# Attention scores from unsplit factors in one run of eight matmuls, and the state step joined to the output step

## The chip, the cores and the metric

The kernel runs on one core of a Trainium2 chip. The metric is the time of one execution in device microseconds, as the median of several runs. TensorE (PE in the profile, PEld for its weight loads) does the matmuls, VectorE (DVE), ScalarE (ACT) and GpSimd (POOL) work on tiles in the on-chip memory, and SyncE (SP) issues the DMAs.

## What is computed

Three layers follow each other: a linear attention with a decaying state, a mixture of four experts weighted by given probabilities, and a second mixture of eight experts to which each row is routed. The change touches the attention alone:

```python
def _attn_ref(r, k, v, w, u) -> np.ndarray:      # batch 4, heads 8, seq 768, head_dim 48
    ...
    for t in range(S):
        kt, vt, rt = (k[:, :, t], v[:, :, t], r[:, :, t])
        cur = np.einsum('bhd,bhe->bhde', u[None] * kt, vt)
        y[:, :, t] = np.einsum('bhd,bhde->bhe', rt, state + cur)
        state = w[None, :, :, None] * state + np.einsum('bhd,bhe->bhde', kt, vt)
```

The first mixture is `p[:, e] * (relu(x @ w1[e]) @ w2[e])` summed over its four experts, for 3072 rows of 384 with a hidden size of 1024.

## The kernel before

**The attention** is done in 24 chunks, six for each of the four batch entries. A chunk is 128 positions of all eight heads, which lie as four pairs; the two heads of a pair lie in the partitions 0 to 63 and 64 to 127 of the transposed factors. `attn_steps` gives the steps of one chunk. `mul` scales the loaded transposed r and k by powers of w, `rk`, `ru`, `kn` and `cv` on POOL and `cc` on DVE make the term with u and the scaled k. `scores` multiplies k by r for each head into two PSUM tiles, `am` (DVE) copies these under the causal mask, `y_mm` multiplies by v and adds the part of the state before, `x_add` (DVE) adds the term with u, `state` makes the next state (four matmuls, then on DVE an addition and a multiplication), and `tr` transposes the chunk's x and splits it on ACT and DVE into the two parts of `XT`, which the first mixture multiplies.

Chunks 0 to 5 take the scores from the factors as they are, in float32 and over the 48 rows of a head: eight matmuls (line 968). The trace shows each of these as two records. Chunks 6 to 23 first split both factors into a high and a low part (`k_parts` on DVE and POOL, `r_parts` on ACT and DVE) and take three products of parts over 64 rows: 24 matmuls (line 963).

**The first mixture** is the bulk of PE's work. It runs as 32 units: for each of 16 pairs of batch entry and expert, two blocks of 384 rows. A unit is `up` (72 matmuls of 384 columns, lines 1133 to 1137, three for each of eight hidden blocks times three) and then `down` (72 more, lines 1154 to 1158). After each hidden block ACT and DVE split the result into the two parts of h (lines 1141, 1142). Unit 0 multiplies the rows of chunks 0 to 2, unit 1 those of chunks 3 to 5.

**What sets the order.** The attention steps are strewn between these matmuls by program order. `tick()` is called after every third matmul, so 48 times in a unit, 24 of them in `up`. Every third tick takes one step from `queue`; in unit 0 a second one is taken on the ticks between while more than 11 steps wait. Chunks 3 to 5 are queued for unit 0. At the start of the units 1 to 6, 9 to 14 and 17 to 22 what is left in the queue is done at once by `flush()`, and one chunk, 6 to 23, is queued. So step number n of such a chunk stands behind tick 3n of its unit: the first behind hidden block 0, the eighth at the end of `up`, the ninth and tenth in `down`. Every engine works through its instructions in this order and waits only for the data.

Of the kernel before, what the change touches and what calls it, by code (L numbers as in the profile page):

```python
# [8 lines left out]
F32 = mybir.dt.float32  # L9
F32R = mybir.dt.float32r  # L10
BF = mybir.dt.bfloat16
I32 = mybir.dt.int32
AF = mybir.ActivationFunctionType
OP = mybir.AluOpType
# [617 lines left out]
def rwkv_moe_moe(ctx, tc, A, out):  # L632
# [104 lines left out]
    with tc.If(chunked > 0) as cmp:  # L737
        main(tc, A, out, C, False)
    with cmp.Else():
        main(tc, A, out, C, True)  # L740
# [74 lines left out]
def main(ctx, tc, A, out, C, stepwise):  # L815
    nc = tc.nc
# [6 lines left out]
    at = att_ctx.enter_context(tc.tile_pool(name="at", bufs=1))  # L823
# [3 lines left out]
    ld = {}  # L827
# [66 lines left out]
    ps = {}  # L894
# [3 lines left out]
    def attn_steps(ck, detail=False):  # L898
        c = ck % 6
        b = ck // 6  # L900
        split_scores = ck >= 6

        def mul(engine, p0=0, p1=4):
            t, n = ld[ck]
            engine.tensor_tensor(t[:, :, p0:p1], t[:, :, p0:p1], tp[:, :, p0:p1, 0:128], op=OP.mult)

        def rk():
            t, n = ld[ck]
            r, k = n[:, 0:384], n[:, 768:1280].rearrange("p (h d) -> p h d", h=8)
            r3 = r.rearrange("p (h d) -> p h d", h=8)  # L910
            nc.gpsimd.tensor_tensor(r3, r3, k[:, :, 0:48], op=OP.mult)

        def ru():
            r = ld[ck][1][:, 0:384]
            nc.gpsimd.tensor_tensor(r, r, u_b, op=OP.mult)

        def kn():
            t, n = ld[ck]
            nc.gpsimd.tensor_tensor(n[:, 768:1280], n[:, 768:1280], pkn.rearrange("p a b -> p (a b)"), op=OP.mult)

        def pre():
            rk()
            ru()
            kn()
# [14 lines left out]
            cc()  # L939
            cv()  # L940


        def k_parts():
            t, n = ld[ck]
            nc.vector.tensor_copy(Kb[:, 0], t[:, 1])
            nc.gpsimd.tensor_tensor(Kb[:, 1], t[:, 1], Kb[:, 0].bitcast(F32), op=OP.subtract)

        def r_parts():
            t, n = ld[ck]
            nc.scalar.activation(Rb[:, 0], t[:, 0], AF.Copy)  # L950
            nc.vector.tensor_sub(Rb[:, 1], t[:, 0], Rb[:, 0].bitcast(F32))

        def scores(p0, p1):
            t, n = ld[ck]
            if p0 == 0:
                ps[ck] = [psum.tile([128, 4, 128], F32, name="at", bufs=4) for _ in range(2)]
            if split_scores:

                for p in range(p0, p1):
                    for n, (a, b) in enumerate(((0, 0), (0, 1), (1, 0))):  # L960
                        for s in range(2):
                            q = slice(64 * s, 64 * s + 64)
                            nc.tensor.matmul(ps[ck][s][:, p, :], Kb[q, a, p], Rb[q, b, p], start=n == 0, stop=n == 2)  # L963
                return
            for p in range(p0, p1):
                for s in range(2):
                    q = slice(64 * s, 64 * s + 48)
                    nc.tensor.matmul(ps[ck][s][:, p, :], t[q, 1, p, :], t[q, 0, p, :], start=True, stop=True)  # L968

        def am(p0=0, p1=4):  # L970
            if p0 == 0:
                st[ck] = at.tile([128, 2, 4, 128], F32, name="am", bufs=1)
            for s in range(2):
                nc.vector.tensor_mul(st[ck][:, s, p0:p1], ps[ck][s][:, p0:p1],
                                     mask[:, None, :].to_broadcast([128, p1 - p0, 128]))

        def att():
            scores(2, 4)
            am()

        def yy():
            y_mm()
            x_add()

        def y_mm():
            t, n = ld[ck]
            v = n[:, 384:768]
            y = psum.tile([128, D], F32, name="at", bufs=4)
            for p in range(4):
                if c:  # L990
                    nc.tensor.matmul(y[:, 96 * p:96 * p + 96], t[:, 0, p, :], S[ck - 1][:, p, :],  # L991
                                     start=True, stop=False)
                for s in range(2):
                    h = 2 * p + s
                    nc.tensor.matmul(y[:, 48 * h:48 * h + 48], st[ck][:, s, p, :],  # L995
                                     v[:, 48 * h:48 * h + 48],
                                     start=not c, stop=bool(s) or not c)
            st[ck] = y

        def x_add():  # L1000
            x = at.tile([128, D], F32, name="x", bufs=2)
            nc.vector.tensor_add(x, st[ck], ld[ck][1][:, 0:384])
            st[ck] = x
# [36 lines left out]
        nothing = lambda: None  # L1040
        if stepwise:
            return [fetch, nothing, nothing, nothing, nothing, nothing, tr]
        if detail:
            return dict(mul=mul, rk=rk, ru=ru, kn=kn, cc=cc, cv=cv, scores=scores, am=am, y=y_mm, x=x_add, state=state, tr=tr)
        if not split_scores:
            return [lambda: (mul(nc.vector), pre()), pre2, lambda: scores(0, 2), att, yy, state, tr]
        return [lambda: mul(nc.gpsimd), k_parts, r_parts, pre, pre2, lambda: scores(0, 2), att, yy, state, tr]

    if not stepwise:
        Rb = at.tile([128, 2, 4, 128], F32R, name="Rb")  # L1050
        Kb = at.tile([128, 2, 4, 128], F32R, name="Kb")


    W1, W2 = {}, {}
# [205 lines left out]
    def enqueue(ck, tail=0):  # L1260
        s = attn_steps(ck)

        def head():
            if 4 <= ck + 1 < NCK:
                load_chunk(ck + 1)
            s[0]()
        queue.append(head)
        queue.extend(s[1:])
# [5 lines left out]
    if stepwise:  # L1274
# [5 lines left out]
        for ck in range(3):  # L1280
            for f in attn_steps(ck):
                f()
        for f in range(8):
            split(1, f, wl[0])
    else:
# [20 lines left out]
        def w128_in():  # L1306
            w128 = C["w128"]
            nc.vector.tensor_mul(w128, tp[:, 0, :, 128:129], tp[:, 0, :, 128:129])
            for s in range(2):
                r = slice(64 * s, 64 * s + 48)  # L1310
                nc.vector.tensor_copy(w128m[r, :, 48 * s:48 * s + 48], w128[r].to_broadcast([48, 4, 48]))

        a, b, c = (attn_steps(ck, True) for ck in range(3))
        a["mul"](nc.gpsimd, 0, 1)
        a["mul"](nc.gpsimd, 1, 2)
# [56 lines left out]
    for ui, (i, blk) in enumerate(units):  # L1372
        b, e = runs[i]
# [204 lines left out]
    for ph in range(E2):  # L1578
        a, b, c = route.phase(ph == E2 - 1, name_job, start_job, 20 if ph == 0 else None)
# [9 lines left out]
    def tick1(j):  # L1589
        clk[0] += 0.161  # L1590
        if len(job) > j + 2:
            return
        due = lambda q: q and clk[0] >= ready[q is search]

        hold = due(search) and not (number and not job)
        if due(number) and (not number[0][1] or not search or len(job) < j + 2 or hold and search[0][1]):
            pop_route(number)
            if hold and search and search[0][1]:
                pop_route(search)
        elif hold:  # L1600
            pop_route(search)

    def tick2(j):
        tick1(j)
        take_names()
        for q in known[j:j + 2]:
            prepare(q, "loads")
        for q in job[j:j + 2]:
            if q["rows"] and rows_there:
                prepare(q, "rows")  # L1610
                break
# [13 lines left out]
    while len(job) < 1 or job[0]["rows"]:  # L1625
        n = min([jb["rows"][0][2]() for jb in job[:1]] + [ready[x is search] for x in (number, search) if x])
# [12 lines left out]
    for j in range(E2):  # L1639
# [27 lines left out]
        t, t1 = lambda: tick2(j), lambda: tick1(j)  # L1667
# [54 lines left out]
```

## Time and profile before

| | |
|---|---|
| median of 3 runs | 1244.8 us (1244.26 to 1245.34) |
| the profiled execution | 1240.1 us, its span in the trace 1238.1 us |
| PE busy | 1213.8 us, 98% of the span |
| VectorE, ScalarE, GpSimd busy | 51%, 23%, 33% |
| the units with a chunk of split scores | 18 of 32 |
| one matmul of 384 columns, start to start | 0.173 us |

A PE that is busy for 98% of the span does not yet say that every microsecond is needed: a busy time is the union of overlapping records, and a record is longer (0.34 us) than the distance to the next (0.17 us). What a step costs on PE is read from starts: from the last matmul of the mixture ahead of it to the second one behind it, less the two distances that would lie there without the step. The second one is taken, because behind a step the first starts, and then the second still comes late.

### The profile page before, as it was taken

The page shows a single profiled execution, that of the slowest core. Times are in us where ns is not written, and L with a number is a line of the kernel's source. Part 1 is how long each engine was busy: PE and PEld are TensorE (multiplying, and loading weights), DVE is VectorE, ACT ScalarE, POOL GpSimd, SP SyncE. Part 2 cuts the span into 40 slices and gives each one's busy share as a digit, 9 for nine tenths or more (in the row PEclk, how much of TensorE's full clock was granted, in tenths as well). Part 3 has the DMA queues.
Part 4 walks back from the last instruction along what each step waited for, and adds up shares of the span by engine and source line. Part 5 has one row for each costly group of instructions (what it writes and reads, how often), then busy time and mean ns, then how long its engine had stood idle before and what let it go on. Part 6 is the DMA issues. An engine that isn't in the chain of part 4 may idle for free.

```text
span 1238.1 us, 21280 instructions
## 1 busy us (share of the span) xinstructions
PE 1213.8 (98%) x7986; PEld 1174.4 (95%) x7986; DVE 629.5 (51%) x1667; ACT 287.2 (23%) x608; POOL 412.0 (33%) x413
## 2 busy tenths in 40 slices
PE   8999999999999999999999999999999999999995
PEld 8899999999999999999999999999998888899995
DVE  7643333367333334863333369279674766663320
ACT  1322222211222222232222222223211011222221
POOL 5555454511444444234444433222200012122210
PEclk7899999999999999999999999999999999999998
DMA  6676555433777777477777655779730486667770
GB/s 250 209 258 241 199 182 201 141 122 121 246 255 256 254 257 258 159 246 272 248 260 251 231 170 172 256 262 317 247 119 18 152 281 230 221 223 267 283 287 27
DMA packets 95929, 267.65 MB, mean 216 GB/s; under 512 B 11328, under 2 KB 15552, under 8 KB 95680
## 3 DMA queue, kind: packets, MB, share of 16 engines
q1 hardware_dynamic: 92736, 256.67, 60.1%
q0 software_dynamic: 3072, 9.44, 2.1%
q8 instruction: 67, 1.10, 0.4%
q14 instruction: 54, 0.44, 0.1%
HBM read 181.13 MB, written 84.93 MB: 215 GB/s over the span
## 4 chain that ended last, share of the span: by engine, by line
PE 89%; issue 4%; DMA 2%; DVE 2%; POOL 1%; ACT 0%; POOLq 0%; DVEq 0%; ACTq 0%
PE mm L1133 13%; PE mm L1154 13%; PE mm L1156 13%; PE mm L1158 13%; PE mm L1135 13%; PE mm L1137 12%; PE at L995 3%; PE at L963 2%; PE at L991 2%; DMA acc<-x2d,idx 1%; PE at L1012 1%; PE at L471 1%; PE at L1028 1%; POOL out_dram L1661 1%; PE at L968 1%
## 5 line engine op out<-in xcount | busy, mean ns | idle before, releaser
L1133 PE MATMUL mm<-xT,w 128*128 128x384 f32 x960 | 327.5, 341 | 0.6 <-ACT xT L1544 0.6
L1135 PE MATMUL mm<-xT,w 128*128 128x384 f32 x960 | 322.8, 336 | 0.2
L1137 PE MATMUL mm<-xT,w 128*128 128x384 f32 x960 | 322.3, 336 | 0.0
L1154 PE MATMUL mm<-w,h 128*128 128x384 f32 x939 | 320.5, 341 | 0.9 <-DMA w<-w2s 0.9
L1156 PE MATMUL mm<-w,h 128*128 128x384 f32 x939 | 315.8, 336 | 0.0
L1158 PE MATMUL mm<-w,h 128*128 128x384 f32 x939 | 315.5, 336 | 0.0
L1141 ACT ACTIVATE h<-mm 128x384 fp32r<-128x384 f32 x313 | 153.9, 492 | 529.2 <-PE mm L1137 487.2
L1142 DVE SCALAR_TENSOR_TENSOR h<-mm,h 128x384 fp32r<-128x384 f32 x313 | 173.7, 556 | 197.1 <-ACT h L1141 195.9
L1073 POOL TENSOR_TENSOR ws<-raw,ws 128x384 fp32r<-128x384 f32 x128 | 135.2, 1062 | 345.3 <-ACT ws L1072 345.2
L1133 PEld LDWEIGHTS mm<-xT,w 128*128 128x128 f32 x960 | 180.3, 188 | 4.4 <-ACT xT L1544 0.8
L1135 PEld LDWEIGHTS mm<-xT,w 128*128 128x128 f32 x960 | 180.4, 188 | 1.2 <-DVE xT L1545 0.8
L1137 PEld LDWEIGHTS mm<-xT,w 128*128 128x128 f32 x960 | 180.3, 188 | 0.1
L1154 PEld LDWEIGHTS mm<-w,h 128*128 128x128 f32 x939 | 176.6, 188 | 1.7 <-ACT ws L1072 1.2
L1156 PEld LDWEIGHTS mm<-w,h 128*128 128x128 f32 x939 | 176.6, 188 | 0.9 <-issue 0.4
L1158 PEld LDWEIGHTS mm<-w,h 128*128 128x128 f32 x939 | 176.3, 188 | 0.4
L1170 DVE SCALAR_TENSOR_TENSOR scr<-acc,wg 128x384 f32<-128x384 f32 x192 | 118.9, 657 | 0.1
L1418 DVE SCALAR_TENSOR_TENSOR acc<-mm,dp,acc 128x384 f32<-128x384 f32 x72 | 44.4, 617 | 105.6 <-PE mm L1158 105.4
L1073 POOL TENSOR_TENSOR w<-raw,w 128x384 fp32r<-128x384 f32 x60 | 61.1, 1039 | 95.6 <-ACT w L1072 95.6
L1072 ACT ACTIVATE ws<-raw 128x384 fp32r<-128x384 f32 x128 | 65.0, 519 | 97.9 <-DMA v2s<-ws 52.5
L1528 POOL DMA_INDIRECT acc<-x2d,idx x24 | 23.7, 988 | 163.9 <-DVE xl L504 112.8
L1661 POOL DMA_INDIRECT out_dram<-acc,idx x24 | 24.3, 1014 | 120.0 <-ACT acc L1659 115.9
L995 PE MATMUL at<-rkv,am 128*128 128x48 f32 x352 | 50.7, 273 | 0.1
(250 smaller groups left out, 1041.6 us busy)
## 6 DMA issues: line engine op xcount, KB each, us to landing
w<-w1s SPq DMA_DIRECT2D x72, 384.0 KB, 4.5
w<-w2s SPq DMA_DIRECT2D x72, 384.0 KB, 6.1
raw<-in_v_dram SPq DMA_DIRECT2D x64, 384.0 KB, 4.5
v1s<-ws SPq DMA_DIRECT2D x64, 384.0 KB, 3.2
v2s<-ws SPq DMA_DIRECT2D x64, 384.0 KB, 3.2
w<-v1s SPq DMA_DIRECT2D x64, 384.0 KB, 6.5
w<-v2s SPq DMA_DIRECT2D x64, 384.0 KB, 5.8
rkv<-in_rkv_dram SPq DMA_DIRECT2D x22, 640.0 KB, 6.7
```

Of the source, the lines that this page charges most:

```text
L995: nc.tensor.matmul(y[:, 48 * h:48 * h + 48], st[ck][:, s, p, :], v[:, 48 * h:48 * h + 48], start=not c, stop=bool(s) or not c)
L1072: nc.scalar.activation(w[:, 0], r, AF.Copy)
L1073: engine.tensor_tensor(w[:, 1], r, w[:, 0].bitcast(F32), op=OP.subtract)
L1133: nc.tensor.matmul(p, w[:, 0, ks], xh, start=(k == 0), stop=False)
L1135: nc.tensor.matmul(p, w[:, 0, ks], xl, start=False, stop=False)
L1137: nc.tensor.matmul(p, w[:, 1, ks], xh, start=False, stop=(k == 2))
L1141: nc.scalar.activation(h[:, 0], p, AF.Relu)
L1142: nc.vector.scalar_tensor_tensor(h[:, 1], p, 0.0, h[:, 0].bitcast(F32), op0=OP.max, op1=OP.subtract)
L1154: nc.tensor.matmul(p, h[:, 0, ts], w[:, 0], start=(f == 0), stop=False)
L1156: nc.tensor.matmul(p, h[:, 0, ts], w[:, 1], start=False, stop=False)
L1158: nc.tensor.matmul(p, h[:, 1, ts], w[:, 0], start=False, stop=(f == FB - 1))
L1170: nc.vector.scalar_tensor_tensor(scr[e % 2], x, 1.0, wg[:, e], op0=OP.mult, op1=OP.mult, accum_out=to[:, e:e + 1])
```

## The change

The split path is gone: `k_parts`, `r_parts`, the tiles `Rb` and `Kb` and the three-product loop are taken out, and every chunk uses line 968's loop. `mul` moves for chunks 6 to 23 from POOL to DVE. All eight matmuls of the scores stand in one step, where they were two steps of two pairs each, and `state` stands right behind `y_mm`, ahead of `x_add`. Three empty steps are put between. So chunks 3 to 5 change too: their scores were in two steps of four matmuls.

```diff
-        split_scores = ck >= 6
...
-        def k_parts():
-            t, n = ld[ck]
-            nc.vector.tensor_copy(Kb[:, 0], t[:, 1])
-            nc.gpsimd.tensor_tensor(Kb[:, 1], t[:, 1], Kb[:, 0].bitcast(F32), op=OP.subtract)
-
-        def r_parts():
-            t, n = ld[ck]
-            nc.scalar.activation(Rb[:, 0], t[:, 0], AF.Copy)
-            nc.vector.tensor_sub(Rb[:, 1], t[:, 0], Rb[:, 0].bitcast(F32))
...
-            if split_scores:
-
-                for p in range(p0, p1):
-                    for n, (a, b) in enumerate(((0, 0), (0, 1), (1, 0))):
-                        for s in range(2):
-                            q = slice(64 * s, 64 * s + 64)
-                            nc.tensor.matmul(ps[ck][s][:, p, :], Kb[q, a, p], Rb[q, b, p], start=n == 0, stop=n == 2)
-                return
             for p in range(p0, p1):
                 for s in range(2):
                     q = slice(64 * s, 64 * s + 48)
...
         def att():
-            scores(2, 4)
+            scores(0, 4)
             am()
 
         def yy():
             y_mm()
+            state()
             x_add()
...
-        if not split_scores:
-            return [lambda: (mul(nc.vector), pre()), pre2, lambda: scores(0, 2), att, yy, state, tr]
-        return [lambda: mul(nc.gpsimd), k_parts, r_parts, pre, pre2, lambda: scores(0, 2), att, yy, state, tr]
-
-    if not stepwise:
-        Rb = at.tile([128, 2, 4, 128], F32R, name="Rb")
-        Kb = at.tile([128, 2, 4, 128], F32R, name="Kb")
+        return [lambda: (mul(nc.vector), pre()), pre2, nothing, att, nothing, yy, nothing, tr]
```

Lines behind the change move up by 25 in the new kernel (1133 is 1108, 1154 is 1129), the attention's by 19 or 20 (968 is 948, 1028 is 1009).

**PE in unit 1**, where chunk 6 is done. Before, the scores stand in two places with a hidden block of `up` between them, the output behind `up`, and the state (line 1012) in `down`:

```order
L963 MATMUL at<-Rb,Kb 128x128 x12
L1133 MATMUL mm<-xT,w_553 128x384
L1135 MATMUL mm<-xT,w_553 128x384
...
L963 MATMUL at<-Rb,Kb 128x128 x12
L1133 MATMUL mm<-xT,w_584 128x384
...
L995 MATMUL at<-rkv_70,am 128x48 x8
L1154 MATMUL mm<-w_484,h 128x384
...
L1012 MATMUL at<-rkv_70 128x96 x4
L1154 MATMUL mm<-w_596,h 128x384
```

And now:

```order
L948 MATMUL at<-rkT_68 128x128 x8
L1108 MATMUL mm<-xT,w_473 128x384
L1110 MATMUL mm<-xT,w_473 128x384
...
L976 MATMUL at<-rkv_70,am 128x48 x8
L993 MATMUL at<-rkv_70 128x96 x4
L1108 MATMUL mm<-xT,w_551 128x384
...
L1009 MATMUL at<-ident,x 128x128 x3
L1129 MATMUL mm<-w_476,h 128x384
```

Four places where PE leaves the mixture for the attention (scores twice, output, state) became two, and all of the chunk lies in `up`.

**PE where unit 0 ends and unit 1 begins.** Before, the transposes of chunk 5 (line 1028) stand nine matmuls ahead of the first matmul of unit 1, which reads what they become:

```order
L1028 MATMUL at<-ident,x 128x128 x3
L1154 MATMUL mm<-w_664,h 128x384
L1156 MATMUL mm<-w_664,h 128x384
L1158 MATMUL mm<-w_664,h 128x384
...
L1158 MATMUL mm<-w_704,h 128x384
L1133 MATMUL mm<-xT,w_366 128x384
```

And now, since chunks 3 to 5 bring 23 steps into unit 0's queue instead of 20 and the last is left to `flush()`:

```order
L1129 MATMUL mm<-w_702,h 128x384
L1131 MATMUL mm<-w_702,h 128x384
L1133 MATMUL mm<-w_702,h 128x384
L1009 MATMUL at<-ident,x 128x128 x3
L1108 MATMUL mm<-xT,w_364 128x384
L1110 MATMUL mm<-xT,w_364 128x384
```

The transposes stand right ahead of their first reader.

**DVE in unit 2**, chunk 7. Before (945 and 951 are the splitting, 974 `am`, 1002 `x_add`, 1016 and 1017 the state, 1031 the end of `tr`):

```order
L945 CAST Kb<-rkT_69 128x512
L1142 SCALAR_TENSOR_TENSOR h<-mm,h 128x384
L951 TENSOR_TENSOR Rb<-rkT_69,Rb 128x512
L1142 SCALAR_TENSOR_TENSOR h<-mm,h 128x384 x2
L930 TENSOR_REDUCE cc<-rkv_71 128x8
...
L974 TENSOR_TENSOR am<-at,mask 128x512 x2
L1142 SCALAR_TENSOR_TENSOR h<-mm,h 128x384
L1002 TENSOR_TENSOR x<-at,rkv_71 128x384
L1016 TENSOR_TENSOR S<-at,S 128x384
L1017 TENSOR_TENSOR S<-S,w128m 128x384
L1031 TENSOR_TENSOR xT<-at,xT 128x3x128
```

And now:

```order
L904 TENSOR_TENSOR rkT_69<-rkT_69,tp 128x1024
L1117 SCALAR_TENSOR_TENSOR h<-mm,h 128x384
L929 TENSOR_REDUCE cc<-rkv_71 128x8
L1117 SCALAR_TENSOR_TENSOR h<-mm,h 128x384 x2
L954 TENSOR_TENSOR am<-at,mask 128x512 x2
L1117 SCALAR_TENSOR_TENSOR h<-mm,h 128x384 x2
L997 TENSOR_TENSOR S<-at,S 128x384
L998 TENSOR_TENSOR S<-S,w128m 128x384
L983 TENSOR_TENSOR x<-at,rkv_71 128x384
L1117 SCALAR_TENSOR_TENSOR h<-mm,h 128x384 x2
L1012 TENSOR_TENSOR xT<-at,xT 128x3x128
```

The scaling of both factors came in, the two steps of splitting went, and the state's two operations now stand ahead of x.

## Rows read from the trace of the kernel before

**Rows 1.** The page: busy times of the engines, and the chain that ended last.

```profile
PE 1213.8 (98%) x7986; PEld 1174.4 (95%) x7986; DVE 629.5 (51%) x1667; ACT 287.2 (23%) x608; POOL 412.0 (33%) x413
PE 89%; issue 4%; DMA 2%; DVE 2%; POOL 1%; ACT 0%; POOLq 0%; DVEq 0%; ACTq 0%
```

**Rows 2.** Timeline of PE, unit 1: start us, length us, line, count [idle before].

```profile
89.97 0.34 PE L1137 MATMUL mm<-xT,w 128*128 128x384 f32 x1
90.23 0.89 PE L963 MATMUL at<-Rb,Kb 64*128 64x128 f32 x12
91.05 0.45 PE L1133 MATMUL mm<-xT,w 128*128 128x384 f32 x1
91.34 0.34 PE L1135 MATMUL mm<-xT,w 128*128 128x384 f32 x1
91.51 0.34 PE L1137 MATMUL mm<-xT,w 128*128 128x384 f32 x1
```

**Rows 3.** Waits over the whole span: us in total, times, longest.

```profile
PEld at L963 <- issue: 9.0, 36, 0.3
```

**Rows 4.** Timeline of PE, unit 0, half of chunk 4's unsplit scores.

```profile
53.95 0.34 PE L1137 MATMUL mm<-xT,w 128*128 128x384 f32 x1
54.22 0.71 PE L968 MATMUL at<-rkT 48*128 48x128 f32 x8
54.86 0.44 PE L1133 MATMUL mm<-xT,w 128*128 128x384 f32 x1
55.14 0.34 PE L1135 MATMUL mm<-xT,w 128*128 128x384 f32 x1
```

**Rows 5.** Timeline of PE before unit 0: chunk 1's eight score matmuls in one run.

```profile
14.14 1.16 PE L968 MATMUL at<-rkT 48*128 48x128 f32 x16
```

**Rows 6.** Timeline of PE, unit 1's `down`: the state of chunk 6.

```profile
98.78 0.34 PE L1158 MATMUL mm<-w,h 128*128 128x384 f32 x1
98.95 1.03 PE L1012 MATMUL at<-rkv 128*128 128x96 f32 x8
99.76 0.42 PE L1154 MATMUL mm<-w,h 128*128 128x384 f32 x1
100.02 0.34 PE L1156 MATMUL mm<-w,h 128*128 128x384 f32 x1
```

**Rows 7.** Groups by line: shapes, count | busy us, mean ns | idle before.

```profile
L905 DVE TENSOR_TENSOR rkT<-rkT,tp 128x1024 f32<-128x1024 f32 x3 | 5.1, 1706 | 0.0
L974 DVE TENSOR_TENSOR am<-at,mask 128x512 f32<-128x512 f32 x46 | 29.4, 682 | 7.7 <-PE at L995 5.3 <-PE at L968 2.4
L1017 DVE TENSOR_TENSOR S<-S,w128m 128x384 f32<-128x384 f32 x16 | 9.5, 592 | 0.6
L1002 DVE TENSOR_TENSOR x<-at,rkv 128x384 f32<-128x384 f32 x22 | 12.3, 557 | 29.9 <-PE at L995 25.0 <-POOL w L1073 4.8
L1142 DVE SCALAR_TENSOR_TENSOR h<-mm,h 128x384 fp32r<-128x384 f32 x313 | 173.7, 556 | 197.1 <-ACT h L1141 195.9
L1141 ACT ACTIVATE h<-mm 128x384 fp32r<-128x384 f32 x313 | 153.9, 492 | 529.2 <-PE mm L1137 487.2 <-DVE scr L1170 37.4 <-DVE h L1142 1.1
L1154 PE MATMUL mm<-w,h 128*128 128x384 f32 x939 | 320.5, 341 | 0.9 <-DMA w<-w2s 0.9
```

**Rows 8.** Timeline, unit 0: chunk 4's scaling on DVE, and its scores waiting.

```profile
50.24 1.93 DVE L905 TENSOR_TENSOR rkT<-rkT,tp 128x1024 f32<-128x1024 f32 x1
...
52.32 0.71 PE L968 MATMUL at<-rkT 48*128 48x128 f32 x8 [1.60 <-DVE rkT L905]
```

**Rows 9.** Timeline, end of unit 0: chunk 5's transposes and what follows them.

```profile
78.89 0.49 PE L1028 MATMUL at<-ident,x 128*128 128x128 f32 x3
...
79.13 0.42 PE L1154 MATMUL mm<-w,h 128*128 128x384 f32 x1
...
79.41 0.49 ACT L1030 ACTIVATE xT<-at 128x384 fp32r<-128x384 f32 x1 [14.69 <-PE at L1028]
...
79.94 0.56 DVE L1031 TENSOR_TENSOR xT<-at,xT 128x384 fp32r<-128x384 f32 x1 [2.83 <-ACT xT L1030]
```

## The prediction

> **What bounds the kernel now.** I read the page first: PE is busy for 98% of the span and makes 89% of the chain that ended last [rows 1]. So time is won or lost where PE's row of matmuls is made shorter or has to wait. Next I read PE's timeline around one attention step, start against start. Between 91.34 and 91.51 the mixture's matmuls follow each other at 0.173 us [rows 2]; this is the yardstick. Twelve records of split scores lie between the start at 89.97 and that at 91.34, so they cost 91.34 - 89.97 - 2 x 0.173 = 1.02 us [rows 2]. Then the waits: the weight loads of line 963 stood idle 36 times, 0.25 us each, and no other engine is named as the cause [rows 3]. There are 18 such chunks with two halves each, so every half pays for coming in, whatever it computes. Four of the same matmuls unsplit, eight records, cost 55.14 - 53.95 - 2 x 0.173 = 0.84 us [rows 4].
>
> **The scores of chunks 6 to 23.** Before, 2 x 1.02 = 2.04 us of PE. Now one run of sixteen unsplit records between the mixture's matmuls. The trace has such a run, of chunk 1: 1.16 us against 0.71 us for eight records [rows 4, 5], so eight more records cost 0.45 us. The new run then costs 0.84 + 0.45 = 1.29 us, and of the 0.84 us some 0.39 us is what coming in and going out cost. Won: 0.75 us a chunk, 18 x 0.75 = 13.5 us. The bounds: if joining two halves saved nothing, the new run would cost 2 x 0.84 = 1.68 us and 18 x 0.36 = 6.5 us would be won; at the other end nothing in these rows would give more than 0.75 us a chunk. I take 0.75, since rows 5 are a run of just this kind, and since each half is seen to pay its own idle time [rows 3].
>
> The Trainium skill bears on this gap: TensorEngine Tiling (Array Packing), under Key Properties, says that a change of the tiling mode drains TensorE, and the heads' matmuls use half of the array's rows. The trace agrees: 0.26 us from the last full matmul to the first of the scores, against 0.17 us between others. By that rule half the changes of mode would mean half the gaps, which is what the sum has anyway.
>
> **The scores of chunks 3 to 5** were already unsplit, in two halves: 3 x (1.68 - 1.29) = 1.2 us won.
>
> **The state behind the output.** Alone in the mixture it costs 100.02 - 98.78 - 2 x 0.173 = 0.89 us. It comes in without a gap (0.17 us), but behind it the second matmul starts 0.26 us after the first, 0.09 us late [rows 6]. Joined to the output, which pays the same behind itself, one such 0.09 us goes. Of the chunks 3 to 22 all but 5, 11 and 17 have a state: 17 x 0.09 = 1.5 us. If the two steps joined badly, this is 0; it cannot be much more than 0.09 each.
>
> **What moves off the path.** POOL loses the scaling and a subtraction, ACT a copy, DVE a copy and a subtraction; PE waited for none of them beyond what stands above, so this wins nothing by itself. DVE gets the scaling, 1.7 us [rows 7]. What hides it: the scores stand nine ticks, 27 matmuls or 4.7 us, behind the first step. In these DVE must wait for hidden block 0 (0.34 us for its last matmul, 0.49 us for ACT's half), do its own half of 0.56 us and then the scaling, in all 0.34 + 0.49 + 0.56 + 1.71 = 3.1 us [rows 2, 7]. There are 1.6 us to spare. Queued behind the scaling on DVE are the h of block 1 and `cc`; PE reads that h only in `down`, six hidden blocks later.
>
> The mask is two operations of 0.68 us [rows 7], 1.4 us and some 0.3 us to start; the output now comes 18 matmuls or 3.2 us after the scores instead of 1.6 us, so this cover grows. x comes behind the state's two operations on DVE: 0.56 + 0.59 + 0.56 = 1.7 us [rows 7] and 0.3 us to start, against the 18 matmuls with their late second, 3.2 us, up to the transposes. There are 1.2 us to spare in every unit from 1 on. POOL's steps (`kn` for the state, `rk`, `ru` for `cc`) stand further ahead of their readers than before, with less queued ahead of them. The loads of the next chunk stay in the first step, so nothing on SP's queue moves but by what PE gains. The first mixture's weights must come some 0.8 us sooner in each unit with a chunk; PE waited for them for 0.9 us in the whole span [rows 7], so I put that at zero.
>
> **What unit 0 pays.** Its queue has 23 steps where it had 20, so three things change there.
> - Chunk 5's transposes stand right ahead of unit 1. In the trace they start at 78.89, the mixture goes on at 79.13, but the low part of XT is done only at 79.94 + 0.56 = 80.50 [rows 9]. Its reader is the second matmul of unit 1, which would start 0.5 us after the transposes and must now wait until 1.6: 1.1 us lost, where nine matmuls covered it before.
> - Chunk 3's x is wanted nine matmuls after the state (here the queue still gives two steps in three ticks), 1.65 us, and takes 2.0 us: 0.4 us lost.
> - Chunk 4's scores waited 1.60 us for the scaling on DVE [rows 8]. Now the scaling stands behind one more h and one more split of weights, but twelve matmuls instead of nine lie before the scores. I leave 1.6 us in place; between 0 and 3.2 is possible.
>
> **The sum.** 13.5 + 1.2 + 1.5 - 1.1 - 0.4 = 14.7 us. The profiled execution took 1240.1 us, 1238.1 of them span, and would come to 1225.4. The median of the runs is 1244.8 us, 4.7 above that one; the sum concerns PE's steps, which do not depend on that, so the forecast is 1244.8 - 14.7 = 1230.1 us. A measurement of this kernel can tell about 0.2%, 2.5 us, from no change.
>
> **Rivals.**
> - *Joining saves nothing.* What a half pays might be the cost of its pairs and not of coming in. Then 6.5 + 0 + 1.5 - 1.5 = 6.5 us are won: 1238.3 us. Against it: 1.16 against 0.71 us [rows 4, 5]. Chance 0.05.
> - *x becomes the late one.* If DVE's three operations take twice their time, as one scaling of 1.93 us against a mean of 1.71 us [rows 7, 8] hints that DVE's times are not fixed, x is ready after 3.7 us, 0.5 us late, in 17 chunks: 8.5 us given back, 1238.6 us; it needs 0.8 us a chunk to eat all. Against it: POOL's work shrinks in the same place. Chance 0.04.
> - *The scaling on DVE holds up every chunk, slower than before.* Chunk 4 shows the price: 1.60 us where twelve records or fewer lie between [rows 8]. If all 18 chunks waited like this, 18 x 1.6 = 28.8 us are lost against 14.7 won: 1258.9 us. It decides from a wait of 0.8 us a chunk on, that is with the scaling done 2.4 us later than worked out above. What could do that is a DVE held up ahead of it, by an accumulation from the unit before. Chance 0.03.
> - *Unsplit products cost more than split ones.* If an unsplit matmul streamed four passes where the split has three, a run would cost 2.04 x 4/3 - 0.39 = 2.33 us, 0.29 us more than before: 5.2 us lost, 1.2 + 1.5 - 1.5 won, 1248.8 us. Against it: two records for a matmul and 0.84 us for a half, measured in the same unit as this mixture [rows 4]. Chance 0.01. The Trainium skill has this rule, four passes for true FP32, in FP8 and Floating Point Precision, under TensorE Precision Notes; the trace shows two records for an unsplit matmul and no cost of four.
> - *Unit 0 is off by more, either way*: nothing lost there and chunk 4's wait gone gives 13.5 + 1.2 + 1.5 + 1.6 = 17.8 us, 1227.0; chunk 4 waiting twice as long and as much again for chunk 3 and 5 gives 14.7 - 1.6 - 1.5 = 11.6 us, 1233.2. This is inside the forecast's case.
>
> **How the numbers follow.** The forecast with its unit 0 has 0.87, the rivals 0.13. The range goes from 1226.5, under the best of unit 0, to 1236, to which the milder half of x being late also belongs. Joining without effect lies outside it. Faster by over 0.2%: the forecast and the first two rivals, less a little for a larger wait by x, 0.94. Within 0.2%: 0.02. Slower: 0.04 from the last two mechanisms.
>
> **What would show it.** Around the new run of line 948: a cost of 1.29 us from start to start, and 16 records. At the transposes of each unit from 1 on: no wait of PE for DVE's x. At the start of unit 1: PE idle about 1.1 us, named for ACT or DVE's XT. The units 2 to 5, 10 to 13 and 18 to 21 should each be 0.75 + 0.09 = 0.84 us shorter than before. The forecast is wrong if waits of PE for `rkT`, `x` or XT come back in every unit, or if the run of sixteen records costs what two halves cost.

## The result and the profile after

| | before, beside it | changed | ratio, 95% interval |
|---|---|---|---|
| median | 1244.53 us | 1230.82 us (4 runs, 1229.44 to 1231.63) | 0.9891 [0.9874, 0.9908] |
| the profiled execution | 1240.1 us, span 1238.1 | 1230.51 us, span 1228.6 | |

By the medians 13.7 us are won, where 14.7 were forecast, and 1230.82 us lies inside the forecast's range of 1226.5 to 1236. Of 38 later executions of the kernel before, two took 1234.38 and 1234.99 us, at a mean granted clock of 0.996 and 0.994 where the others had 0.983 to 0.989, so single times are not compared, only medians and steps. The two profiled executions differ by 9.6 us only. Between the starts of units 0 and 26 the new kernel is 12.9 us shorter. It lost 0.9 us ahead of unit 0, where both kernels have the same instructions on PE, and 2.5 us behind unit 25, where the change touches nothing; unit 31 took 61.9 us in this execution and 60.4 before, and 60.2 in a second profile of the same kernel (below). So the steps are compared one by one, start to start, as in the prediction; the two distances between matmuls that are taken off come to 0.347 us.

The page of the changed kernel, against [rows 1]:

```profile
PE 1202.2 (98%) x7842; PEld 1168.0 (95%) x7842; DVE 624.4 (51%) x1649; ACT 277.2 (23%) x590; POOL 350.0 (28%) x377
PE 90%; issue 4%; DMA 2%; DVE 1%; POOL 1%; ACT 0%; SPq 0%; POOLq 0%; ACTq 0%
```

PE is still busy for 98%, with 11.6 us less to do. POOL lost 62 us of work; what that had to do with PE stands with the mask in the part on the prediction.

**The scores.** Timeline of PE in unit 1 after the change, chunk 6 (start us, length us, engine, line; the columns of all timelines here). Line 948 is the scores, 1108 to 1112 are `up`, 1129 to 1133 `down`:

```profile
88.49 0.34 PE L1112 MATMUL mm<-xT,w 128*128 128x384 f32 x1
88.76 1.16 PE L948 MATMUL at<-rkT 48*128 48x128 f32 x16
89.85 0.45 PE L1108 MATMUL mm<-xT,w 128*128 128x384 f32 x1
90.13 0.34 PE L1110 MATMUL mm<-xT,w 128*128 128x384 f32 x1
```

Sixteen records in a run cost 90.13 - 88.49 - 0.347 = 1.29 us; over all 18 chunks the mean is 1.297. The 36 split halves before cost 36.7 us together, 1.02 us each as the one in [rows 2]. So 36.7 - 18 x 1.297 = 13.4 us are won here, and 1.2 us in chunks 3 to 5, where six halves of 0.85 became three runs of 1.297.

**The state behind the output.** Chunk 7 is the cleanest, since nothing waits there. Timeline of PE and PEld before; lines 991 and 995 are the output, 1012 the state:

```profile
125.46 0.34 PE L1137 MATMUL mm<-xT,w 128*128 128x384 f32 x1
125.63 0.36 PE L991 MATMUL at<-S,rkT 128*128 128x96 f32 x2
...
127.84 0.57 PE L995 MATMUL at<-rkv,am 128*128 128x48 f32 x4
128.23 0.42 PE L1154 MATMUL mm<-w,h 128*128 128x384 f32 x1
128.49 0.34 PE L1156 MATMUL mm<-w,h 128*128 128x384 f32 x1
...
129.71 0.34 PE L1158 MATMUL mm<-w,h 128*128 128x384 f32 x1
129.71 1.03 PEld L1012 LDWEIGHTS at<-rkv 128*128 128x128 f32 x8
129.88 1.03 PE L1012 MATMUL at<-rkv 128*128 128x96 f32 x8
130.69 0.42 PE L1154 MATMUL mm<-w,h 128*128 128x384 f32 x1
130.95 0.34 PE L1156 MATMUL mm<-w,h 128*128 128x384 f32 x1
```

And after, where 972 and 976 are the output and 993 the state:

```profile
122.21 0.34 PE L1112 MATMUL mm<-xT,w 128*128 128x384 f32 x1
122.38 0.36 PE L972 MATMUL at<-S,rkT 128*128 128x96 f32 x2
...
124.59 0.57 PE L976 MATMUL at<-rkv,am 128*128 128x48 f32 x4
124.95 0.97 PEld L993 LDWEIGHTS at<-rkv 128*128 128x128 f32 x8
124.99 1.10 PE L993 MATMUL at<-rkv 128*128 128x96 f32 x8
125.87 0.42 PE L1108 MATMUL mm<-xT,w 128*128 128x384 f32 x1
126.13 0.34 PE L1110 MATMUL mm<-xT,w 128*128 128x384 f32 x1
```

Before: 128.49 - 125.46 - 0.347 = 2.68 us for the output and 130.95 - 129.71 - 0.347 = 0.89 us for the state, 3.58 in all. After: 126.13 - 122.21 - 0.347 = 3.57 us. One late second matmul did go, and still nothing was won. In such a run of short matmuls the weight loads start 0.11 us apart, and so do the matmuls: the state's eight records take 0.88 us (124.99 to 125.87). Alone, the first of these loads runs beside the mixture's last matmul, 0.17 us ahead of its own (129.71 against 129.88), and the eight take only 0.81 us (129.88 to 130.69). Joined, the load comes 0.04 us ahead (124.95 against 124.99) and hides behind nothing. What the exit gives back, the entry takes. The costs say the same: 0.89 us for 8 records, 2.68 for 24 and 3.57 for 32 are all 0.112 us a record, wherever the records stand. That it is the loads that set this pace is read from the starts; no run changes the loads alone.

**Unit 0 and the start of unit 1.** Waits of PE after, from unit 0's start to unit 1's end (us in all, times, longest). Before, the first of them was the only one there, with the same 1.6:

```profile
PE at L948 <- DVE rkT L904: 1.6, 1, 1.6
PE mm L1108 <- ACT xT L1011: 0.6, 1, 0.6
PE at L1009 <- DVE x L983: 0.2, 1, 0.2
```

Where unit 1 starts, behind chunk 5's transposes (line 1009; 1011 and 1012 make the two parts of `XT`), against [rows 9]:

```profile
80.65 0.34 PE L1133 MATMUL mm<-w,h 128*128 128x384 f32 x1
...
80.83 0.49 PE L1009 MATMUL at<-ident,x 128*128 128x128 f32 x3
...
81.35 0.49 ACT L1011 ACTIVATE xT<-at 128x384 fp32r<-128x384 f32 x1 [14.78 <-PE at L1009]
81.88 0.56 DVE L1012 TENSOR_TENSOR xT<-at,xT 128x384 fp32r<-128x384 f32 x1 [0.23 <-ACT xT L1011]
...
81.89 0.44 PE L1108 MATMUL mm<-xT,w 128*128 128x384 f32 x1 [0.58 <-ACT xT L1011]
82.49 0.19 PEld L1110 LDWEIGHTS mm<-xT,w 128*128 128x128 f32 x1 [0.41 <-DVE xT L1012]
82.49 0.44 PE L1110 MATMUL mm<-xT,w 128*128 128x384 f32 x1
```

The transposes cost 82.49 - 80.65 - 0.347 = 1.49 us here, against 0.33 us where nobody waits: 1.16 us lost. The wait list shows only 0.6 of it, since the rest is in the weight load behind. Chunk 3's x costs 0.40 us in the same way. Chunk 4's scores cost 2.96 us where others cost 1.30, so they wait 1.67 us, as before [rows 8].

### The profile page after: what moved, and what is told of

It reads as the page before. It is cut to its first block, busy times and chain, and to the rows that moved or that the text cites. A ratio compares the mean times of both kernels' runs of the same rounds, so it can differ in the third digit from the quotient of the medians.

```text
span 1228.6 us, 20929 instructions
## 1 busy us (share of the span) xinstructions
PE 1202.2 (98%) x7842; PEld 1168.0 (95%) x7842; DVE 624.4 (51%) x1649; ACT 277.2 (23%) x590; POOL 350.0 (28%) x377
## 3 DMA queue, kind: packets, MB, share of 16 engines
q1 hardware_dynamic: 92736, 256.67, 60.5%
## 4 chain that ended last, share of the span: by engine, by line
PE 90%; issue 4%; DMA 2%; DVE 1%; POOL 1%; ACT 0%; SPq 0%; POOLq 0%; ACTq 0%
PE mm L1108 13%; PE mm L1131 13%; PE mm L1110 13%; PE mm L1129 13%; PE mm L1133 13%; PE mm L1112 13%; PE at L976 4%; PE at L948 2%; PE at L972 2%; PE at L993 2%; DMA acc<-x2d,idx 1%; PE at L471 1%; PE at L1009 1%; POOL out_dram L1636 1%; PE at L598 0%
```

## The experiments

The first four undo or do one part at a time; they ran on one chip, beside 17 runs of the kernel before (median 1243.12 us). The others stand beside 14 runs (1243.31) or, the last two, beside 7 (1244.68). Behind each time stands its ratio to these runs, with a 95% interval. What a step costs is read from the one profile of each run.

**Only the state joined**, on the kernel before:

```diff
-        return [lambda: mul(nc.gpsimd), k_parts, r_parts, pre, pre2, lambda: scores(0, 2), att, yy, state, tr]
+        return [lambda: mul(nc.gpsimd), k_parts, r_parts, pre, pre2, lambda: scores(0, 2), att,
+                lambda: (y_mm(), state(), x_add()), nothing, tr]
```

> The kernel before, with one part of the change: for chunks 6 to 23 the state stands right behind the output, its own step is empty. First theory (the prediction's): alone the state pays 0.09 us behind itself, joined it does not, so output and state together fall from 2.68 + 0.89 = 3.58 us to 3.49 us and 15 chunks give 1.3 us. Second theory, formed on the trace of the changed kernel: in a run of short matmuls the weight loads set the pace, 0.112 us each; alone, the first of them is loaded under the mixture's matmul and wins what the end then loses, so joining gives 0.00 us a chunk and the time does not change: 1244.5 us.

1241.54 us, 0.9986 [0.9966, 1.0005]. The output and the state cost 3.576 us in one run, 3.577 in two. The time alone could not decide, since the first theory's 1.3 us would be a ratio of 0.9990, which the interval holds as well as 1; the steps decide for the second theory: joining gives nothing, as in chunk 7 above.

**Only the products changed**: unsplit factors in the two old halves, and k and r split no longer.

```diff
-            if split_scores:
+            if False:
...
-        return [lambda: mul(nc.gpsimd), k_parts, r_parts, pre, pre2, lambda: scores(0, 2), att, yy, state, tr]
+        return [lambda: mul(nc.gpsimd), nothing, nothing, pre, pre2, lambda: scores(0, 2), att, yy, state, tr]
```

> The kernel before, with chunks 6 to 23 taking their scores from the unsplit factors, still in two steps of four matmuls; the scaling stays on GpSimd, the splitting is left out. Theory: half the gain is the smaller number of records: a half falls from 1.02 to 0.85 us, 36 halves give 6.1 us, 1238.4 us. Rival: all of the gain is from joining and nothing comes from leaving out the split: 1244.5 us. Rival: all of it is from unsplit factors, 13 us.

1235.33 us, 0.9938 [0.9925, 0.9951]. A half costs 0.851 us instead of 1.02, so 36 x 0.17 = 6.1 us of PE. By the medians it is 7.8 us, with 6.1 at the low end of the interval; another 0.5 us of it is a wait for the mask that ended (see the part on the prediction).

**Only the halves joined**: the split products in one run.

```diff
-        return [lambda: mul(nc.gpsimd), k_parts, r_parts, pre, pre2, lambda: scores(0, 2), att, yy, state, tr]
+        return [lambda: mul(nc.gpsimd), k_parts, r_parts, pre, pre2, lambda: (scores(0, 4), am()), nothing, yy, state, tr]
```

> The kernel before, with the split scores of chunks 6 to 23 in one run of 24 matmuls instead of two of 12; all else as it was. Theory: coming in and going out are paid once: 0.35 + 12 x 0.112 = 1.69 us instead of 2.04, 18 chunks give 6.3 us, 1238.2 us. Rival: the cost belongs to the matmuls and not to coming in: no change, 1244.5 us.

1235.56 us, 0.9938 [0.9925, 0.9951]. Its run, line 963, in unit 1:

```profile
87.41 0.34 PE L1137 MATMUL mm<-xT,w 128*128 128x384 f32 x1
87.67 1.55 PE L963 MATMUL at<-Rb,Kb 64*128 64x128 f32 x24
89.16 0.44 PE L1133 MATMUL mm<-xT,w 128*128 128x384 f32 x1
89.44 0.34 PE L1135 MATMUL mm<-xT,w 128*128 128x384 f32 x1
```

89.44 - 87.41 - 0.347 = 1.68 us for 24 records, where two runs of 12 cost 2.04: 0.36 us a chunk, 6.4 us in 18 (7.6 by the medians, with 6.1 at the low end of the interval). Twice the records add 0.055 us each here ((1.685 - 1.020) / 12) and 0.056 us each with unsplit factors ((1.297 - 0.851) / 8), so what is left for coming in and going out is 0.36 us with split and 0.40 us with unsplit ones. From the two unsplit halves of the run before this one, 30.6 us, to one run a chunk, 23.3 us, joining wins 7.3 us, and with the 6.1 us of the products that makes the 13.4.

**What a run pays for coming in and going out**: the changed kernel with the scores of chunks 6 to 23 over whole rows.

```diff
-                    q = slice(64 * s, 64 * s + 48)
+                    q = slice(64 * s, 64 * s + 48) if ck < 6 else slice(0, 128)
```

> The changed kernel, with the scores of chunks 6 to 23 multiplied over all 128 rows of the array instead of 48 of one half, so that both heads of a pair are added up in each product: that changes what is computed, eight matmuls a chunk stay. Theory: the 0.39 us of a run of scores is paid for changing between whole and half rows. Then a run over whole rows pays nothing for coming in, but its records no longer go in pairs: 16 x 0.112 = 1.79 us against 1.30, 18 x 0.49 = 8.8 us slower than the changed kernel, 1239.6 us. Rival: any interruption of the mixture costs 0.39 us: 2.18 us a run, 15.8 us slower, 1246.6 us.

1236.63 us, 0.9947 [0.9929, 0.9964]. Its run in unit 1:

```profile
87.35 0.34 PE L1112 MATMUL mm<-xT,w 128*128 128x384 f32 x1
87.53 1.95 PE L948 MATMUL at<-rkT 128*128 128x128 f32 x16
89.23 0.42 PE L1108 MATMUL mm<-xT,w 128*128 128x384 f32 x1
89.49 0.34 PE L1110 MATMUL mm<-xT,w 128*128 128x384 f32 x1
```

16 records cost 89.49 - 87.35 - 0.347 = 1.79 us, 0.112 each and nothing for coming in and going out: the first starts 0.18 us behind the mixture, not 0.27. That is 0.49 us a chunk more than in the changed kernel, 8.8 us in 18, as expected; the changed kernel was not run beside this one, so the steps and not the times are compared. So the 0.36 to 0.40 us are paid where matmuls of half the rows and of all rows follow each other, and the records of half the rows go in pairs, two in 0.11 us. The Trainium skill's TensorEngine Tiling (Array Packing), Key Properties, says that a change of the tiling mode drains TensorE; the runs agree in that the change of rows costs time, and show how much, but not that a drain is what takes it.

**The changed kernel once more**, to see which part of its first profile was the execution's own.

> The changed kernel once more, beside the three below. Its first profile lost 2.5 us against the kernel before in the parts behind the first mixture and 0.9 us ahead of unit 0, where no instruction of PE differs. Theory: these are differences between executions; the units 0 to 25 are again 12.9 us shorter than before, and the time is 13.0 to 13.7 us under the kernel before. Rival: the change costs something in the routing part (unit 31, 61.9 us against 60.4 before); then the 61.9 us come again.

1227.82 us, 0.9881 [0.9856, 0.9905]. The same costs step by step, units 0 to 25 are 13.0 us shorter than before, and unit 31 takes 60.2 us, so its 61.9 us belonged to one execution. The time missed what was expected: 15.5 us under the kernel before and not 13.0 to 13.7, though the interval, 11.8 to 17.9 us, holds these.

**The scaling back on POOL** for chunks 6 to 23:

```diff
-        return [lambda: (mul(nc.vector), pre()), pre2, nothing, att, nothing, yy, nothing, tr]
+        return [lambda: (mul(nc.vector if ck < 6 else nc.gpsimd), pre()), pre2, nothing, att, nothing, yy, nothing, tr]
```

> The changed kernel with the scaling of chunks 6 to 23 back on GpSimd. Theory: it is off the path on either engine, since 27 matmuls lie between it and the scores: 0.0 us, 1230.8 us, no wait of PE ahead of the scores. Rival: GpSimd, held behind the splitting of the second mixture's weights, makes the scores wait: up to 1 us a chunk in the units 9 to 22, 12 us slower.

1228.94 us, 0.9884 [0.985, 0.9918]: no difference from the changed kernel beside it (1227.82 us) that these runs can tell. The run of scores costs 1.297 us either way. Where the scaling runs decides nothing here; on either engine it is done ahead of the scores.

**How much cover x needs**: for chunks 6 to 23 the empty step between output and transposes is taken out, so that 9 matmuls stand there instead of 18.

```diff
+        if ck >= 6:
+            return [lambda: (mul(nc.vector), pre()), pre2, nothing, att, nothing, yy, tr]
```

> The changed kernel without the empty step between output and transposes in chunks 6 to 23: nine matmuls of cover for x instead of 18. Theory: x comes behind the state's two operations on DVE, 1.7 us and some 0.3 us to start, against 1.65 us; PE waits 0.4 us as for chunk 3, in the 12 chunks whose state has two operations: 4.8 us slower, 1235.6 us. In the three chunks with one operation and the three without a state no wait. Rival: x does not wait for the state's operations in any way that PE sees: 0.0 us, 1230.8 us.

1233.68 us, 0.9928 [0.9907, 0.9948], 5.9 us above the changed kernel beside it. DVE and PE of this run in unit 2; 997, 998 and 983 are the state's two operations and x:

```profile
127.22 0.56 DVE L997 TENSOR_TENSOR S<-at,S 128x384 f32<-128x384 f32 x1 [2.46 <-PE at L993]
127.81 0.56 DVE L998 TENSOR_TENSOR S<-S,w128m 128x384 f32<-128x384 f32 x1
128.28 0.55 DVE L983 TENSOR_TENSOR x<-at,rkv 128x384 f32<-128x384 f32 x1
128.98 0.52 PE L1009 MATMUL at<-ident,x 128*128 128x128 f32 x3 [0.20 <-DVE x L983]
```

The transposes cost 0.73 us instead of 0.33 in 12 chunks, and over all chunks 13.3 us instead of 8.5: 4.8 us. In the profiled execution another 1.3 us are unit 0's (last section). So x can become the late one, by its place behind the state and not by slower operations as the prediction's rival had it, and its price of 0.4 us a chunk is the one expected of this run; 18 matmuls keep it out.

**Unit 0 put right, first try**: two steps of cover for chunk 4's scaling, x ahead of the state, and a step before the transposes.

```diff
+        if ck < 6:
+            yx = lambda: (y_mm(), x_add())
+            head = lambda: (mul(nc.vector), pre())
+            return {3: [head, pre2, att, nothing, yx, state, tr],
+                    4: [head, pre2, nothing, nothing, att, yx, state, tr],
+                    5: [head, pre2, att, yx, nothing, tr]}[ck]
```

> The changed kernel with other lists of steps for chunks 3 to 5 alone, so that unit 0's queue has 20 steps again: chunk 3 has no empty step ahead of its scores and x ahead of the state, chunk 4 two empty steps ahead of its scores, chunk 5 one step less. Theory: the three waits of unit 0 go, 1.16 us at the start of unit 1 for chunk 5's XT, 0.40 us for chunk 3's x, 1.67 us for chunk 4's scaling: 3.2 us, less up to 0.3 us for outputs that now stand nearer to their mask; 3.0 us under the changed kernel, 1227.8 us. Rival: another wait takes their place in unit 0, and less than 1 us is won.

1229.25 us, 0.9895 [0.9868, 0.9922], nothing won. All three waits are gone, and another stands in their place. PE's wait of this run in units 0 and 1, and DVE ahead of it:

```profile
PE at L976 <- DVE am L954: 1.9, 2, 1.7
```

```profile
54.98 0.24 DVE L887 TENSOR_REDUCE psm<-dp 128x24 f32<-128x96 f32 x1
55.26 0.36 DVE L888 TENSOR_SCALAR psm<-psm 128x24 f32<-128x24 f32 x1
55.65 0.30 DVE L889 RECIPROCAL psm<-psm 128x24 f32<-128x24 f32 x1
55.99 0.66 DVE L890 TENSOR_TENSOR dp<-dp,psm 128x96 f32<-128x96 f32 x1
56.57 1.27 DVE L954 TENSOR_TENSOR am<-at,mask 128x512 f32<-128x512 f32 x2
```

Four small operations on the given probabilities `dp`, which program order puts at that point of unit 0, now stood ahead of chunk 4's mask, and the output waited for it. From 60.5 to 63.9 us, 3 us behind this wait, the granted clock was 0.51 (1.2 GHz) and on either side 1.00 (2.4 GHz). Units 0 and 1 took 73.36 us, against 72.71 in the changed kernel beside it. This version traded one wait for another.

**Unit 0, second try**: chunk 4's scaling is done on POOL during chunk 3, and the rest stays in its old distance.

```diff
+        if ck < 6:
+            yx = lambda: (y_mm(), x_add())
+            t4 = lambda: ld[4][0]
+            early = lambda: nc.gpsimd.tensor_tensor(t4(), t4(), tp[:, :, :, 0:128], op=OP.mult)
+            return {3: [lambda: (mul(nc.vector), pre()), pre2, att, early, yx, state, tr],
+                    4: [pre, nothing, att, pre2, yx, state, tr],
+                    5: [lambda: (mul(nc.vector), pre()), pre2, att, nothing, yx, nothing, tr]}[ck]
```

> The changed kernel with other lists for chunks 3 to 5 again, 20 steps for unit 0: chunk 3 has x ahead of the state, chunk 4's scaling is done on GpSimd six ticks earlier and its mask stands ahead of the constants made behind hidden block 5, chunk 5 has one step less. Theory: the waits of unit 0 and at the start of unit 1 are only a matter of what stands where; without them the units 0 and 1 together take 72.7 - 3.2 = 69.5 us, and the time is 3 us under the changed kernel beside it (1227.8 us there), about 1224.8 us. Rival: as in the first try, DVE in unit 0 is full and another wait takes their place; then the units 0 and 1 stay over 71.5 us.

It ran beside the changed kernel:

> The changed kernel on the same chip as the run above, to compare with: 1227 to 1231 us, the units 0 and 1 together 72.7 us.

1228.08 us, 0.9868 [0.9852, 0.9885], against 1231.39 us, 0.9895 [0.9879, 0.9912], for the changed kernel: 3.3 us less. POOL and PE of this run in unit 0, chunk 4 (1029 is the scaling):

```profile
41.87 2.19 POOL L1029 TENSOR_TENSOR rkT<-rkT,tp 128x1024 f32<-128x1024 f32 x1
```

```profile
49.81 1.16 PE L948 MATMUL at<-rkT 48*128 48x128 f32 x16
```

The scaling is done 5.7 us ahead of its reader (41.87 + 2.19 = 44.06 against 49.81), and PE waits for nothing in units 0 and 1. These take 69.21 us instead of 72.49: 3.3 us, which are the three waits of 1.67, 1.16 and 0.40 us. The time expected, 1224.8 us, was missed, because the changed kernel took 1231.39 us on this chip and not 1227.8; the difference of 3 us held, and no run of one reaches into the runs of the other (1226.73 to 1229.65 against 1231.26 to 1232.58 us). Of the versions tried this one has the lowest ratio to the kernel before.

## Why the prediction held, and where its sum was off

- *The scores, 13.5 us*: 13.4. The run of chunk 1 [rows 5] was the right model: 1.29 us expected, 1.297 found, and the runs of 8, 12, 16 and 24 records confirm that entry and exit are paid once a run. *Joining saves nothing* fell with the run of 24.
- *Chunks 3 to 5, 1.2 us*: 1.2.
- *The state, 1.5 us*: 0.0. This is the term that was mis-sized. The prediction counted what stands behind the state, the 0.09 us of [rows 6], and not how it comes in. The prediction's own lower bound, "if the two steps joined badly, this is 0", is what happened; the run with the state alone shows it.
- *What moves off the path "wins nothing by itself"*: 0.5 us won, so this step of the prediction was wrong in a small term. Before, the output had waited for the mask in units 1, 3 and 5, for 0.30, 0.08 and 0.16 us; chunk 6 is one, its output costing 2.08 us where 1.79 is usual. In just these units DVE stood 3.1 to 3.2 us at `cc`, waiting for POOL's `ru` (line 915), against 1.5 us or less in the other units from 2 on, and the mask came behind it. Timeline of DVE before, unit 1:

```profile
92.99 0.55 DVE L930 TENSOR_REDUCE cc<-rkv 128x8 f32<-128x384 f32 x1 [3.13 <-POOL rkv L915]
...
94.39 1.28 DVE L974 TENSOR_TENSOR am<-at,mask 128x512 f32<-128x512 f32 x2
```

  After the change `cc` never waits and no output does. The longer cover alone is not what did it: with only the halves joined the mask had 18 matmuls ahead of its reader, `cc` waited 3.13 us as before, and chunk 6's output still paid 0.16 us; with only the products changed the cover was the old one, `cc` waited 2.41 us, and no output waited. Which part of the splitting's work, on POOL or on DVE, had made the mask late is not separated.
- *Unit 0, -1.1 and -0.4 us*: -1.16 and -0.40. Chunk 4's wait stayed at 1.6 us, as taken.
- *x becomes the late one*: no transposes wait for x from unit 1 on. *The scaling on DVE holds up every chunk*: no chunk from 6 on waits, and moving it back to POOL changes nothing. *Unsplit products cost more*: a half fell from 1.02 to 0.85 us. The Trainium skill's four passes for true FP32 (FP8 and Floating Point Precision, TensorE Precision Notes) show in no run here as a cost: an unsplit matmul is two records, and 0.055 and 0.056 us a record are the price of split and unsplit ones. What passes a record holds the trace does not tell.

With what was measured the sum is 13.4 + 1.2 + 0.0 + 0.5 - 1.16 - 0.4 = 13.5 us. The medians of the three comparisons gave 13.7, 15.5 and 13.3 us. The units 0 to 25 alone are 12.9, 13.0 and 13.3 us shorter in the three profiles; the 0.2 to 0.6 us to the sum are not assigned, and most of them lie in units 0 and 1. So the scores' term was right by its mechanism, and that the time came out 0.7 us from the forecast owes something to luck: 1.5 us too much stood against 0.5 us left out, and the comparisons differ by 2 us. The units with a chunk were forecast 0.84 us shorter; most are 0.73, which is the scores alone, and units 3 and 5 are 0.80 and 0.89, since there the mask's wait went too.

## What to carry to other kernels

Read what a step costs on a pipelined TensorE from start to start, and on both sides: what a join gives back at the exit it may take at the entry, where a first weight load loses the matmul that hid it. Half-row matmuls between full-row ones belong in as few runs as possible, since the change of rows is paid by the run and not by its length. Who moves a step to end a wait has to read its new neighbours on every engine too, because the next wait can be longer than the one removed.

## What the runs showed of the hardware

- Records of short matmuls of whole rows follow each other at 0.112 us, with 48, 96 or 128 columns alike (the output, the state, the scores over whole rows), and their weight loads start at the same distance. Those of half the rows go two in that time.
- Coming from whole rows to half rows and back costs 0.36 to 0.40 us together, of which 0.1 us shows as a gap ahead of the run (0.27 us from start to start instead of 0.17).
- A wait of PE can be followed by a lower clock, and need not. Chunk 4's wait of 1.60 us stands in the kernel before and in all three profiles of the changed one, with the clock at 1.00 (2.4 GHz) behind it. In the run without a step before the transposes the same wait was followed by 3.4 us at 0.5 (1.2 GHz), and unit 0 took 44.2 us instead of 42.9. Stretches of that run (us, busy us of each engine, granted clock, DMA share, GB/s):

```profile
50.00:55.00 5.00, 3.40 (x24) 3.11 (x24) 4.26 (x7) 2.63 (x6) 4.87 (x4) 1.00 0.99 375
55.70:59.10 3.40, 3.40 (x13) 3.38 (x12) 1.82 (x4) 0.90 (x2) 2.69 (x4) 0.50 0.00 0
59.50:65.00 5.50, 5.50 (x45) 5.50 (x44) 2.92 (x7) 0.90 (x2) 1.53 (x2) 1.00 0.25 89
```

  What decides between the two stays open. So the wait cost 1.6 us in most profiles and 2.9 us in this one. A lower clock also came in unit 31, which the change doesn't touch: in the profile of the second try for unit 0 it was at 0.50 there for one such stretch, in the changed kernel's beside it too, and unit 31 took 63.3 us in both. In the others it took 60.1 to 60.4 us, save 61.9 in the first profile of the changed kernel, where the clock was 1.00 throughout and PE's waits in the routing (lines 471 and 502) came to 2.6 us instead of 0.6 in its second profile; why is open.

```profile
966.10:969.50 3.40, 3.39 (x34) 3.03 (x34) 1.88 (x10) 0.49 (x1) 0.00 (x0) 0.50 0.69 209
```

- The start of unit 0 lies between 35.5 and 39.0 us in profiles whose PE does the same until there, so two single executions can differ by 3 us for no reason of the change. The clock goes with it: from 35.2 to 37.0 us it was already 1.00 in the profile with the halves joined, whose unit 0 starts at 35.5, and still 0.50 in the first profile of the changed kernel, whose unit 0 starts at 39.0.
